# Start addresses of the token tiles inside SBUF: from a multiple of 128 bytes to 96 bytes past one

## The chip, the core and the metric

The kernel runs on one core of a Trainium2 chip. The time is the device time of one launch in microseconds (us), from all inputs in DRAM to the output in DRAM; three timed runs of the kernel before give 595.99 us (median; 595.70 to 596.36).

## What is computed

Sliding-window attention (window 64) over 2 x 8 heads of 576 tokens, then a dense mixture of four experts weighted by given probabilities, then a second mixture of eight experts of which each token uses one:

```python
attn = softmax(mask(q @ k.T / 8)) @ v                  # window of 64 tokens, head_dim 64
x = attn as (1152 tokens, 512)
for e in range(4):  out += p[:, e:e+1] * (relu(x @ w1[e]) @ w2[e])        # 512 -> 1024 -> 512
# second mixture: one expert of eight for each token
logits = out @ w_gate + modality_bias[modality_id]; e_idx = argmax(logits)
y[e_idx == e] = gate_w * (relu(out[e_idx == e] @ m2w1[e]) @ m2w2[e])
```

All inputs are float32.

## The kernel before

Every large product is done in three matmuls on values split in two float32r parts (a rounded high part and the rest): high by high, low by high, high by low. Such a product is called a triple here. The tokens lie transposed in two tiles, `xh` (high) and `xl` (low), each [128, 4, 1152]: four blocks of 128 features, 1152 tokens, 4608 bytes for one block's row in a partition. The weights of the expert in work lie in the tiles `wh0` to `wh7` and `wl0` to `wl7` (0 to 3: first layer, 4 to 7: second), 4096 bytes each in a partition; the rows of the first layer's output lie in `hh` and `hl`, [128, 8, 384].

The first layer (`mm1_part`, line 343) streams tokens through TensorE: the stationary operand is a 128-column piece of a weight tile, the moving operand is `xh` or `xl` at one feature block and 256, 352 or 384 tokens. One output block of 128 takes four triples, that is 12 matmuls, in one PSUM bank; ScalarE and VectorE then make `hh` and `hl` of it (lines 352 and 353). The second layer (`mm2_part`, line 368) has 128 (or 96) rows of `hh` or `hl` as the stationary operand and 512 columns of a second-layer weight tile as the moving operand; it doesn't touch `xh` or `xl`.

The program has these stages: attention for 18 blocks of 64 tokens in each sequence, into whose TensorE work the first tokens of expert 0 are mixed (0 to 155 us); the groups of 384 tokens of experts 1 to 3, first layer then second layer (155 to 452 us); the routed slots of 256 and 352 tokens (to the end), whose tokens are gathered, turned and written into `xh` and `xl` again (`turn`, lines 1030 to 1035). The attention writes `xh` and `xl` at lines 330 and 335. In one early piece (`g0_mm`, line 499, 24 matmuls) `xh` and `xl` are the stationary operand.

Tiles are placed one behind the other in each partition, in the order in which a pool first names them, rounded up to 32 bytes. `const` comes first and holds `ident`, `mk`, `prob` and `psumw`; `big` follows with `xh`, `xl`, `hh`, `hl`, `acc` and `ident4`; then `wp` with the weights. Where a tile begins is thus set by the sizes of those ahead of it; the odd widths of `psumw` (24 floats for 9) and `ident4` (56 for 32) are of that kind.

Of the kernel before, what the change touches and what calls it, by code (L numbers as in the profile page):

```python
# [5 lines left out]
F32 = mybir.dt.float32  # L6
# [9 lines left out]
def build(tc, q, k, v, probs, w1, w2, mid, wg, mbias, m2w1, m2w2, out):  # L16
# [4 lines left out]
    NTILE = NT // 128  # L21
# [7 lines left out]
    with ctx:  # L29
        const = ctx.enter_context(tc.tile_pool(name="const", bufs=1))  # L30
        big = ctx.enter_context(tc.tile_pool(name="big", bufs=1))
# [10 lines left out]
        ident = const.tile([128, 128], F32, name="ident")  # L42
        mk = const.tile([128, 3, 128], F32, name="mk")
        prob = const.tile([128, NTILE, E], F32, name="prob")
        psumw = const.tile([128, 24], F32, name="psumw")[:, 0:NTILE].rearrange("p (t o) -> p t o", o=1)
        xh = big.tile([128, HP, NT], F32R, name="xh")
        xl = big.tile([128, HP, NT], F32R, name="xl")
        hh = big.tile([128, KF, GT], F32R, name="hh")
        hl = big.tile([128, KF, GT], F32R, name="hl")
        acc = big.tile([128, NTILE, 520], F32, name="acc")  # L50

        ident4 = big.tile([128, 56], F32, name="ident4")[:, 0:32]

        with tc.manual_schedule():

# [7 lines left out]
            for i2, own in ((0, 0), (1, 1)):  # L63
                a = mk[64 * i2:64 * i2 + 64]
                o, p_ = a[:, :, 64 * own:64 * own + 64], a[:, :, 64 - 64 * own:128 - 64 * own]
# [131 lines left out]
            def unit_of(n):  # L197
                u, hp = divmod(n, HP)
                return units[u] + (u, hp)
# [403 lines left out]
            for n in range(NA):  # L603
                t, nb, u, hp = unit_of(n)
# [676 lines left out]
```

## Time and profile before

| | us |
|---|---|
| median of three runs | 595.99 |
| the profiled execution, its own time | 595.89 |
| its span, first to last instruction | 594.1 |
| TensorE busy in the span | 585.4 (99%) |
| VectorE, ScalarE, GpSimd busy | 248.6, 192.1, 83.4 |
| first-layer matmuls, line 343 | 1632 |
| second-layer matmuls, line 368 | 1104 |

TensorE is busy nearly the whole span. A matmul's busy time in the rows holds its latency too, and matmuls overlap, so the sum of their durations is far over the span; what one costs in a dense stretch is the distance from its start to the next one's start, called its pitch here. Rows of a timeline give starts to 0.01 us, so a pitch is read over several matmuls.

### The profile page before, as it was taken

The numbers are of one execution on the slowest core, as the hardware profiler recorded it, in microseconds if no ns is written. First come the engines' busy times: TensorE is split into PE (matmuls) and PEld (weight loads), VectorE is DVE, ScalarE is ACT, GpSimd is POOL, SyncE is SP. The second block draws the span as 40 slices with busy tenths as digits, with TensorE's granted clock in tenths as the row PEclk, the third lists the DMA queues.
The fourth block names the chain that finished last, engine by engine and source line by source line (L and its number), as shares of the span: only waits on it lengthen the run. The fifth ranks groups of instructions, "written<-read, shape, count | busy, mean of one in ns | idle before, by whom it ended". The sixth has DMA issues, their size and how long they took to land. (4 is left out here: it accounts for less than half of the span.)

```text
span 594.1 us, 9420 instructions
## 1 busy us (share of the span) xinstructions
PE 585.4 (99%) x3818; PEld 517.0 (87%) x3818; DVE 248.6 (42%) x534; ACT 192.1 (32%) x373; POOL 83.4 (14%) x129
## 2 busy tenths in 40 slices
PE   8999999999999999999999999999999999999996
PEld 7798797979898989899898989899898989897964
DVE  4954545363462212524121243335168597233410
ACT  5853434352340101313020222222043455233421
POOL 3851212022000000000000000000002105323221
PEclk9999999999999999999999999999999999999999
DMA  8996460000521000224000040002306277316530
GB/s 212 201 254 99 89 196 1 2 2 1 143 76 68 0 1 0 75 67 135 9 0 1 1 142 1 0 1 69 127 2 203 79 269 210 133 54 207 189 90 31
DMA packets 55919, 51.11 MB, mean 86 GB/s; under 512 B 41151, under 2 KB 41151, under 8 KB 55872
## 3 DMA queue, kind: packets, MB, share of 16 engines
q1 hardware_dynamic: 53664, 45.05, 27.7%
q0 software_dynamic: 1680, 5.29, 2.6%
q8 instruction: 31, 0.51, 0.4%
q10 hardware_dynamic: 528, 0.13, 0.1%
q14 instruction: 16, 0.13, 0.1%
HBM read 45.71 MB, written 4.95 MB: 85 GB/s over the span
## 5 line engine op out<-in xcount | busy, mean ns | idle before, releaser
L343 PE MATMUL ps<-xh,wh 128*128 128x384 f32 (+2 forms) x544 | 173.5, 319 | 0.0
L343 PE MATMUL ps<-xh,wl 128*128 128x384 f32 (+2 forms) x544 | 171.7, 316 | 0.0
L343 PE MATMUL ps<-xl,wh 128*128 128x384 f32 (+2 forms) x544 | 171.5, 315 | 0.0
L368 PE MATMUL ps<-wh,hh 128*128 128x512 f32 (+1 forms) x368 | 147.2, 400 | 0.3 <-DVE hl L353 0.3
L368 PE MATMUL ps<-wh,hl 128*128 128x512 f32 (+1 forms) x368 | 144.0, 391 | 0.0
L368 PE MATMUL ps<-wl,hh 128*128 128x512 f32 (+1 forms) x368 | 143.8, 391 | 0.0
L352 ACT ACTIVATE hh<-ps 128x384 fp32r<-128x384 f32 (+2 forms) x112 | 52.0, 464 | 260.4 <-PE ps L343 255.8
L353 DVE SCALAR_TENSOR_TENSOR hl<-ps,hh 128x384 fp32r<-128x384 f32 (+2 forms) x112 | 58.2, 522 | 118.6 <-ACT hh L352 118.6
L343 PEld LDWEIGHTS ps<-xh,wh 128*128 128x128 f32 x544 | 103.0, 189 | 0.9 <-issue 0.3
L343 PEld LDWEIGHTS ps<-xl,wh 128*128 128x128 f32 x544 | 103.0, 189 | 0.5
L343 PEld LDWEIGHTS ps<-xh,wl 128*128 128x128 f32 x544 | 102.9, 189 | 0.0
L368 PEld LDWEIGHTS ps<-wh,hh 128*128 128x128 f32 (+1 forms) x368 | 68.8, 187 | 16.7 <-issue 2.2
L368 PEld LDWEIGHTS ps<-wh,hl 128*128 128x128 f32 (+1 forms) x368 | 68.7, 187 | 15.3
L368 PEld LDWEIGHTS ps<-wl,hh 128*128 128x128 f32 (+1 forms) x368 | 68.8, 187 | 13.3
L379 DVE SCALAR_TENSOR_TENSOR acc<-ps,prob,acc 128x512 f32<-128x512 f32 x27 | 20.3, 750 | 94.9 <-PE ps L368 94.9
L1019 POOL DMA_INDIRECT xr<-x2d,idg x11 | 12.5, 1137 | 317.5 <-DVE ids L730 314.9
L171 DVE TENSOR_TENSOR wl<-raw,wh 128x1024 fp32r<-128x1024 f32 x42 | 52.0, 1253 | 8.8 <-ACT wh L167 8.8
L167 ACT ACTIVATE wh<-raw 128x1024 fp32r<-128x1024 f32 x48 | 49.1, 1052 | 0.0
L277 ACT ACTIVATE sm<-sm,st 128x128 f32<-128x128 f32 x72 | 23.2, 391 | 5.4 <-DVE st L266 5.4
L294 POOL TENSOR_TENSOR sm<-sm,rs 128x512 f32<-128x512 f32 (+1 forms) x20 | 19.5, 976 | 26.3 <-DVE rs L287 24.3
L257 DVE SCALAR_TENSOR_TENSOR sm<-psS,mk 128x256 f32<-128x256 f32 (+1 forms) x40 | 14.0, 391 | 19.0 <-PE psS L245 17.7
L1042 POOL DMA_INDIRECT out_dram<-y,ids x11 | 11.3, 1024 | 58.5 <-ACT y L1040 37.2
(189 smaller groups left out, 413.1 us busy)
## 6 DMA issues: line engine op xcount, KB each, us to landing
raw<-in_moe_w_dram SPq DMA_DIRECT2D x60, 512.0 KB, 4.0
x2d<-acc SPq DMA_DIRECT2D x3, 780.0 KB, 3.8
va<-in_v_dram SPq DMA_DIRECT2D x8, 256.0 KB, 5.1
vb<-in_v_dram SPq DMA_DIRECT2D x16, 128.0 KB, 4.5
acc<-in_moe_w_dram SPq DMA_DIRECT2D x4, 512.0 KB, 8.6
acc<-in_q_dram SPq DMA_DIRECT2D x6, 128.0 KB, 4.3
qu<-in_q_dram SPq DMA_DIRECT2D x3, 256.0 KB, 4.0
ku<-in_k_dram SPq DMA_DIRECT2D x3, 256.0 KB, 4.8
```

The source lines that it names most:

```text
L167: nc.scalar.activation(out=hi, in_=x, func=ACTF.Copy)
L171: eng.tensor_tensor(out=lo[:, o], in0=x[:, o], in1=hi[:, o].bitcast(F32), op=ALU.subtract)
L257: nc.vector.scalar_tensor_tensor(out=p[:, h], in0=ps[:, h, 0:128 * nj].rearrange("p (j c) -> p j c", j=nj), scalar=0.125, in1=m, op0=ALU.m ...
L277: nc.scalar.activation(out=p[:, h, j], in_=p[:, h, j], func=ACTF.Exp, bias=st[:, o:o + 1])
L294: nc.gpsimd.tensor_tensor(out=p, in0=p, in1=rs.rearrange("p (h j) o -> p h j o", h=2).to_broadcast([128, 2, nj, 128]), op=ALU.mult)
L343: nc.tensor.matmul(out=ps[:, 0:n], lhsT=a[kk][:, fs], rhs=b_[:, kk, gs], start=(kk == 0 and term == 0) if first is None else (first and te ...
L352: nc.scalar.activation(out=hi, in_=ps[:, 0:n], func=ACTF.Relu)
L353: nc.vector.scalar_tensor_tensor(out=lo, in0=ps[:, 0:n], scalar=0.0, in1=hi.bitcast(F32), op0=ALU.max, op1=ALU.subtract)
L368: nc.tensor.matmul(out=ps[0:m], lhsT=a[:, f, ts_], rhs=b_[c][:, o:o + 512], start=(f == 0 and i == 0), stop=(f == KF - 1 and i == 2))
L379: nc.vector.scalar_tensor_tensor(out=o, in0=ps, scalar=prob[:, t, e:e + 1], in1=o, op0=ALU.mult, op1=ALU.add)
L1019: nc.gpsimd.indirect_dma_start(out=x, out_offset=None, in_=x2d[0:last, :], in_offset=bass.IndirectOffsetOnAxis(ap=idg[i][:, a:a + 1], axis=0))
L1042: nc.gpsimd.indirect_dma_start(out=out, out_offset=bass.IndirectOffsetOnAxis(ap=ap, axis=0), in_=y[0:m], in_offset=None, bounds_check=NT - ...
```

## The change

No instruction is added, removed or moved: the lists of instructions of the two programs have the same operations, shapes, waits and order on every engine. Four lines change sizes of tiles, or the place of `ident4`, and with them the addresses. Byte offsets of the tiles in a partition, and what is left of them after the last multiple of 128:

| tile | before | rest | after | rest |
|---|---|---|---|---|
| xh | 18816 | 0 | 18912 | 96 |
| xl | 37248 | 0 | 37344 | 96 |
| hh | 55680 | 0 | 55936 | 0 |
| hl | 67968 | 0 | 68224 | 0 |
| acc | 80256 | 0 | 80512 | 0 |
| ident4 | 98976 | 32 | 55776 | 96 |
| wh0 (the other 15 follow, 4096 apart) | 99200 | 0 | 99328 | 0 |

All tiles behind the weights move on by 128 bytes, as they do. Inside `xh` and `xl` a feature block is 36 times 128 bytes and a group of tokens begins at a multiple of 128 tokens, so every first-layer matmul's moving operand begins at a multiple of 128 before, and 96 bytes past one after. Modulo 512 all of `xh`, `xl`, `hh`, `hl` and the weights begin at the same place (384) before; after, `xh` and `xl` begin at 480, `hh` and `hl` at 128, the weights at 0.

```diff
-        psumw = const.tile([128, 24], F32, name="psumw")[:, 0:NTILE].rearrange("p (t o) -> p t o", o=1)
+        psumw = const.tile([128, 48], F32, name="psumw")[:, 0:NTILE].rearrange("p (t o) -> p t o", o=1)
         xh = big.tile([128, HP, NT], F32R, name="xh")
         xl = big.tile([128, HP, NT], F32R, name="xl")
+
+        ident4 = big.tile([128, 40], F32, name="ident4")[:, 0:32]
         hh = big.tile([128, KF, GT], F32R, name="hh")
         hl = big.tile([128, KF, GT], F32R, name="hl")
-        acc = big.tile([128, NTILE, 520], F32, name="acc")
-
-        ident4 = big.tile([128, 56], F32, name="ident4")[:, 0:32]
+        acc = big.tile([128, NTILE * 520 + 24], F32, name="acc")[:, 0:NTILE * 520].rearrange("p (t d) -> p t d", d=520)
```

Tiles that already begin off a multiple of 128 in the kernel before are useful for reading the rows: token tile t of `acc` begins 32 t bytes past one (2080 bytes each), the gathered rows `xr` begin at 0, 32, 64 or 96 past one, `fewy` at 64 past one, the four feature blocks of `wgb` that line 767 streams at 0, 48, 96 and 16 past one.

## Rows read from the trace of the kernel before

**Rows 1.** The page: span, and busy time, share and instructions of each engine.

```profile
span 594.1 us, 9420 instructions
PE 585.4 (99%) x3818; PEld 517.0 (87%) x3818; DVE 248.6 (42%) x534; ACT 192.1 (32%) x373; POOL 83.4 (14%) x129
```

**Rows 2.** Waits of TensorE: who, for whom, us in total, times, longest.

```profile
PE psW L80 <- POOL ident L57: 1.4, 1, 1.4
PE psX L303 <- POOL sm L294: 0.6, 1, 0.6
PE psS L245 <- DVE sm L257: 0.5, 2, 0.3
PE ps L368 <- DVE hl L353: 0.3, 1, 0.3
```

**Rows 3.** Groups by shape, TensorE: operands, count, busy us, mean ns, idle before.

```profile
L368 PE MATMUL ps<-wh,hh 128*128 128x512 f32 x352 | 140.8, 400 | 0.3 <-DVE hl L353 0.3
L343 PE MATMUL ps<-xh,wh 128*128 128x384 f32 x288 | 97.5, 339 | 0.0
L343 PE MATMUL ps<-xh,wh 128*128 128x256 f32 x192 | 55.3, 288 | 0.0
L343 PE MATMUL ps<-xh,wh 128*128 128x352 f32 x64 | 20.8, 325 | 0.0
```

**Rows 4.** Windows, line 343: length, busy and count of PE and PEld, clock, DMA.

```profile
163.09:177.65 14.56, 14.56 (x85) 14.40 (x84) 1.00 0.29 76
```

**Rows 5.** Timeline of TensorE, 256 tokens then 352 tokens: start us, us, what.

```profile
38.76 0.28 PE L343 MATMUL ps<-xh,wl 128*128 128x256 f32 x1
...
41.64 0.28 PE L343 MATMUL ps<-xh,wl 128*128 128x256 f32 x1
...
517.54 0.32 PE L343 MATMUL ps<-xh,wh 128*128 128x352 f32 x1
...
521.41 0.32 PE L343 MATMUL ps<-xh,wh 128*128 128x352 f32 x1
...
529.57 0.32 PE L343 MATMUL ps<-xh,wh 128*128 128x352 f32 x1
...
531.49 0.39 PE L368 MATMUL ps<-wh,hh 128*128 128x512 f32 x1
```

**Rows 6.** Timeline of TensorE in a second layer, 512 columns.

```profile
385.82 0.39 PE L368 MATMUL ps<-wh,hl 128*128 128x512 f32 x1
...
387.18 0.39 PE L368 MATMUL ps<-wh,hl 128*128 128x512 f32 x1
```

**Rows 7.** Single lines: engine, operation, count, duration ns min/median/max, first and last start.

```profile
L1136 PE MATMUL psF<-acc,xg x16: 592/593/617, 564.8 to 566.2; 128*32 128x512 f32 x16
L1164 PE MATMUL psF<-fewy,ident x2: 592/604/617, 577.7 to 578.1; 128*32 128x512 f32 x2
L767 PE MATMUL psGL<-wgb,xg x108: 172/173/188, 399.4 to 474.5; 128*128 128x24 bf16 x108
L751 PE MATMUL psGT<-ident,acc x36: 270/273/308, 394.3 to 469.8; 128*128 128x128 f32 x36
```

**Rows 8.** Single lines: loads of stationary operands, VectorE on `acc`, writes of token tiles.

```profile
L751 PEld LDWEIGHTS psGT<-ident,acc x36: 138/140/143, 394.1 to 469.7; 128*128 128x128 f32 x36
L1030 PEld LDWEIGHTS psT<-ident,xr x40: 138/139/144, 460.1 to 539.0; 128*128 128x128 f32 x40
L379 DVE SCALAR_TENSOR_TENSOR acc<-ps,prob,acc x27: 745/751/752, 183.3 to 467.7; 128x512 f32<-128x512 f32 x27
L343 PEld LDWEIGHTS ps<-xh,wh x544: 186/188/203, 35.9 to 564.1; 128*128 128x128 f32 x182
L335 DVE TENSOR_TENSOR xl<-psO,xh x20: 259/424/425, 17.0 to 139.0; 128x256 fp32r<-128x256 f32 x16, 128x128 fp32r<-128x128 f32 x4
L1034 ACT ACTIVATE xh<-psT x10: 591/598/600, 461.0 to 539.4; 128x512 fp32r<-128x512 f32 x10
```

**Rows 9.** Timeline of TensorE: a first-layer matmul, then transposes of `acc`, tiles 0 and 3.

```profile
394.10 0.34 PE L343 MATMUL ps<-xh,wl 128*128 128x384 f32 x1
394.28 0.60 PE L751 MATMUL psGT<-ident,acc 128*128 128x128 f32 x4
...
429.86 0.34 PE L343 MATMUL ps<-xh,wl 128*128 128x384 f32 x1
430.03 0.60 PE L751 MATMUL psGT<-ident,acc 128*128 128x128 f32 x4
```

## The prediction

> **What bounds the kernel now.** I read the page first: TensorE is busy 585.4 of 594.1 us, VectorE 248.6, ScalarE 192.1 [rows 1]. Then the waits of TensorE: four pairs, 2.8 us in all, and none of them a first-layer matmul [rows 2]. So the end follows TensorE's own pace, and a nanosecond on a matmul is a nanosecond on the time. The groups by shape name the two big users, line 368 with 512 columns and line 343 with 384, 256 and 352 [rows 3]; their mean durations (400, 339, 288 and 325 ns) contain latency that the next matmul covers, so I take pitches instead. For 384 tokens, 84 matmuls fill 14.56 us: 173.3 ns, at a granted clock of 1.00, the 2.4 GHz level [rows 4]. For 256 tokens, 24 matmuls stand between the first two rows of [rows 5]: 2.88 us / 24 = 120.0 ns. For 512 columns, 6 matmuls in 1.36 us: 226.7 ns [rows 6]. At 2.4 GHz the columns alone are 160.0, 106.7 and 213.3 ns. What is left is the same each time, **13.3 ns**, whatever the width and whichever layer: it is a cost per matmul, not per column, and equals 32 columns, or 128 bytes of a float32r row. For 352 tokens (columns alone 146.7 ns) there are two paces: 24 matmuls in 3.87 us, 161.3 ns, and later, in the same slot and on the same addresses, 12 in 1.92 us, 160.0 ns, again 13.3 over the columns [rows 5].
>
> **The change, part by part.** *Instructions*: none is added, removed or moved, no queue is passed, no wait is new. What changes is where operands start: the moving operand of all 1632 first-layer matmuls (544 triples), the outputs of the instructions that write `xh` and `xl`, and the stationary operand of 24 early matmuls. `hh`, `hl`, `acc`, the weights and everything behind stay on the same rest modulo 128.
>
> *Writes into the token tiles.* 30 on ScalarE and 30 on VectorE over the whole program (20 at lines 330 and 335 each, 10 at lines 1034 and 1035 each) [rows 8]. The nearest row is line 379: its 27 instructions read and write `acc` tiles that begin 0, 32, 64 and 96 past a multiple of 128, and all of them take 745 to 752 ns [rows 8]. At most 7 ns each, so 60 x 7 ns = 0.4 us if all of it were on the path; most of it lies beside TensorE. I take 0. The bound below is -0.4 us by the same row.
>
> *Stationary operands.* 36 loads from `acc` tiles at four rests take 138 to 143 ns, 40 loads from gathered rows at four rests 138 to 144 ns [rows 8]. So 24 x 6 ns = 0.1 us at most, hidden beside the matmul before. I take 0.
>
> *The moving operand*, the term that decides. No row shows a float32r stream that begins off a multiple of 128, so I bound it. From near: line 1164 streams 512 float32 columns from `fewy`, 64 past a multiple, and takes 592 and 617 ns; line 1136 streams 512 from `acc`, on a multiple, and takes 592 to 617 ns [rows 7]: equal at both ends, difference 0. Line 767 streams from four starts, 0, 16, 48 and 96 past a multiple, and its 108 matmuls have one median, 173 ns [rows 7]; these are only 24 bf16 columns, so that row is weak. The first row is stronger, but a plain float32 stream takes two passes and so may have slack that a float32r stream at one column a cycle lacks. From far: the 13.3 ns is the only fixed cost that rows show. It could double (one more piece of 32 columns: +13.3 ns) or fall to what the transposes show. Four of them, 128 columns in two passes (106.7 ns), fill 0.60 us [rows 9], of which the last one takes 0.27 [rows 7]: 0.33 us for three steps, a pitch of 110 ns, 3.3 ns over the columns. That would be -10.0 ns. So the term lies between 1632 x -10.0 ns = **-16.3 us** and 1632 x +13.3 ns = **+21.8 us**. I take **0**, by line 1164, the only row with a long stream off the multiple.
>
> *Relative place of moving and stationary operand.* All large tiles begin at the same place modulo 512 before; afterwards a first-layer stream begins 480 past its weights. One row has that very distance: the matmul at 429.86 streams `xh` while `acc` tile 3 is loaded for the transposes, 480 apart modulo 512, and the next start is 0.17 us later; at 394.10, before `acc` tile 0 with the same start modulo 512, it is 0.18 us [rows 9]. No difference beyond the rows' 0.01 us. I take 0 here too. For the second layer (1104 matmuls) the distance changes by 128 and the rest modulo 128 does not; I take 0.
>
> *Sum*: 595.89 us for the profiled execution (594.1 of span and 1.8 around it) + 0 + 0 + 0 = 595.9, against a median of 595.99 in the timed runs. I predict 596.0.
>
> **Rivals.** *One more piece (slower).* The constant equals 128 bytes for four widths, all of them multiples of 32 columns. If a stream is fetched in pieces of a fixed grid, and the constant is the piece that must be there ahead, a stream that begins 96 past a grid line touches one piece more. With 128-byte pieces that is 13.3 ns on each of 1632 matmuls, +21.8 us, 617.7; with 64-byte pieces half, +10.9 us, 606.8. For it: the exactness of the constant. Against it: line 1164 at 64 past shows nothing [rows 7]. It decides as soon as the 384 pitch exceeds 173.3 by 0.75 ns, since 1632 x 0.75 ns is 1.2 us. By the Trainium skill (SBUF — State Buffer, Specifications (TRN2)) the lines are of 16 bytes, and 96 bytes are six whole ones, so this rival would be worth nothing; no row here shows the size of a line.
>
> *The pace slips (slower, small).* At 352 tokens the stream can stay at 161.3 ns instead of 160.0 [rows 5]. So the 13.3 is a state into which the stream of loads and the stream of columns fall, and not always. If an odd start keeps the other widths out of it in the same way, 1440 matmuls x 1.3 ns = 1.9 us: 597.9. For it: those two paces. Against it: the 256 and 384 streams hold theirs, and 352 found it too after a break.
>
> *The constant shrinks (faster).* If the 13.3 ns comes from loads and streams that begin on the same place modulo 512 and get in each other's way, then moving the tokens apart frees part of it: down to the transposes' 3.3 ns it is -16.3 us, 579.6; half of it, 587.7. For it: a load of 188 ns runs beside every first-layer matmul, one of 140 beside a transpose [rows 8], and the transpose has the smaller rest. Against it: the distance of 480 in [rows 9], which didn't help. The Trainium skill (TensorE: Matmul & The Clock Gate, Back-to-back issue gap) states N/2.4 + 2.5 ns for a matmul alone, which is an estimate of 10.8 ns less than the rows have, and by it the gain could be 17.6 us and the time 578.3; but the same page (Step-by-step: what each phase is for) gives loads a read port of their own, by which they take nothing from the stream.
>
> **How the numbers follow.** No effect: 0.48, 595.5 to 596.5. The pace slips: 0.12, near 597.9. One more piece: 0.19, of which 0.10 for the half (606.8) and 0.09 for the whole (617.7). The constant shrinks: 0.21, of which 0.11 for half (587.7) and 0.10 for the whole (579.6). The range leaves out both whole cases, 0.19, and takes in the half ones with the 0.4 us of the writes and the spread of the runs: 587 to 609. The likeliest case alone would be 595.5 to 596.5. Less than 0.2%, 1.2 us, is about what a measurement of this kernel can't tell from no change: so faster 0.21, same 0.48, slower 0.12 + 0.19 = 0.31.
>
> **What would show it.** In the trace after, the pitch of first-layer matmuls decides: 173.3 ns at 384 tokens and 120.0 at 256 if I am right, 180 to 187 and 127 to 133 for one more piece, 163 to 168 and 110 to 115 if the constant shrinks, and about 174.6 and 121.3 where the pace slips. The second layer is the control, 226.7 ns: if it moves, it is not the start of the tokens that matters but the distance of the tiles. TensorE's waits should stay near 2.8 us; if they grow, the writes into the token tiles got slower, which I hold for the least likely of all. I am wrong if a pitch moves although line 1164 didn't feel its start, which would mean that a one-pass stream has no slack for it.

## The result: 0.6% slower, by the second layer

The changed kernel takes 599.61 us (median of four runs, 598.88 to 600.12) against 595.88 for the kernel before: a ratio of 1.006, 95% interval 1.0043 to 1.0078. That is slower by 3.7 us, on a forecast of no effect (596.0) with a range of 587 to 609.

The page after, the lines that answer to [rows 1], and then TensorE's waits (who, for whom, us in total, times, longest), which answer to [rows 2]:

```profile
span 598.3 us, 9420 instructions
PE 589.6 (99%) x3818; PEld 517.2 (86%) x3818; DVE 248.6 (42%) x534; ACT 192.2 (32%) x373; POOL 83.4 (14%) x129
```

```profile
PE psW L80 <- POOL ident L57: 1.4, 1, 1.4
PE psX L303 <- POOL sm L294: 0.6, 1, 0.6
PE psS L245 <- DVE sm L257: 0.5, 2, 0.3
PE ps L368 <- DVE hl L353: 0.4, 1, 0.4
```

The instructions are the same, and the busy time of VectorE, ScalarE and GpSimd and the waits are the same to 0.1 us. Only TensorE is busy 4.2 us longer, the whole of the span's growth. The groups of TensorE after (line, operands, count, then busy us and mean ns), and behind them two groups of the page before, say which matmuls:

```profile
L343 PE MATMUL ps<-xh,wh 128*128 128x384 f32 (+2 forms) x544 | 173.6, 319 | 0.0
L343 PE MATMUL ps<-xl,wh 128*128 128x384 f32 (+2 forms) x544 | 171.5, 315 | 0.0
L343 PE MATMUL ps<-xh,wl 128*128 128x384 f32 (+2 forms) x544 | 171.2, 315 | 0.0
L368 PE MATMUL ps<-wh,hh 128*128 128x512 f32 (+1 forms) x368 | 148.6, 404 | 0.4 <-DVE hl L353 0.4
L368 PE MATMUL ps<-wh,hl 128*128 128x512 f32 (+1 forms) x368 | 145.3, 395 | 0.0
L368 PE MATMUL ps<-wl,hh 128*128 128x512 f32 (+1 forms) x368 | 145.1, 394 | 0.0
```

```profile
L368 PE MATMUL ps<-wh,hh 128*128 128x512 f32 (+1 forms) x368 | 147.2, 400 | 0.3 <-DVE hl L353 0.3
L368 PE MATMUL ps<-wh,hl 128*128 128x512 f32 (+1 forms) x368 | 144.0, 391 | 0.0
```

The first layer, whose tokens were moved by 96 bytes, is where it was to 0.5 us in these rows. The second layer, which touches neither token tile, is slower in all three terms: its mean is 394 to 404 ns for 391 to 400 before. In dense stretches (runs of matmuls with nothing else between them) the pitch shows it plainly. The windows of the kernel after (length, then busy time and count of TensorE and of its loads; first a second layer of 60 matmuls, then first layers of 84 with 384 tokens and 84 with 256; TensorE's count holds a neighbour or two that overlap the edge):

```profile
214.48:228.43 13.95, 13.95 (x61) 11.12 (x59) 1.00 0.01 1
197.14:211.70 14.56, 14.56 (x85) 14.40 (x84) 1.00 0.00 0
140.50:150.44 9.94, 9.94 (x86) 9.90 (x84) 1.00 0.01 2
```

The same second layer and the same first layer of 256 tokens in the kernel before:

```profile
213.44:227.04 13.60, 13.60 (x61) 11.08 (x59) 1.00 0.00 1
140.00:150.07 10.07, 10.07 (x86) 10.03 (x84) 1.00 0.01 2
```

13.95 us / 60 = **232.5 ns**, against 13.60 / 60 = 226.7 before, as in [rows 6]; 14.56 / 84 = 173.3 ns, the same as [rows 4]; 9.94 / 84 = 118.3 ns, against 120.0 in [rows 5]. Summed from start to start over all rows of the two traces, line 368 grew by 4.6 us (4.1 ns on each of 1104 matmuls; the pitch in stretches that are cut by other matmuls grew less), line 343 shrank by 1.0 us (256 tokens -0.8, 352 -0.2, 384 -0.05), and the first layer began 0.6 us later, a delay that arose in the first 15 us, while the inputs come in. 4.6 - 1.0 + 0.6 = 4.2 us, the growth of the span. The last part may be of that one execution alone: the medians differ by 3.7 us, and in the traces of the other kernels the first layer begins anywhere from 35.3 to 36.6 us.

So the start of the tokens did not cost anything where it was looked for, and something that the change moved on the way did: `hh` and `hl` by 256 bytes, the weights by 128. Both stay on multiples of 128, but modulo 256 the second layer's moving operand (a weight tile) now begins 128 past its stationary one (`hh` or `hl`), where before the two began on the same place.

### The profile page after: what moved, and what is told of

Its sections match the earlier page's. It is cut to its first block, busy times and chain, and to the rows that moved or that the text cites. A ratio compares the mean times of both kernels' runs of the same rounds, so it can differ in the third digit from the quotient of the medians.

```text
span 598.3 us, 9420 instructions
## 1 busy us (share of the span) xinstructions
PE 589.6 (99%) x3818; PEld 517.2 (86%) x3818; DVE 248.6 (42%) x534; ACT 192.2 (32%) x373; POOL 83.4 (14%) x129
## 5 line engine op out<-in xcount | busy, mean ns | idle before, releaser
L171 POOL TENSOR_TENSOR wl<-raw,wh 128x1024 fp32r<-128x1024 f32 x6 | 14.4, 2408 | 34.7 <-ACT wh L167 34.7
```

The source lines that it names most:

```text
L171: eng.tensor_tensor(out=lo[:, o], in0=x[:, o], in1=hi[:, o].bitcast(F32), op=ALU.subtract)
```

## Experiments: distance or start?

Two theories. **A**: the pace goes by the distance between the starts of a matmul's moving and stationary operand, modulo some power of two up to 512. **B**: it goes by where a tile itself begins. All kernels below compute the same with the same instructions; they differ from the kernel before in padding alone, and each diff shows only the lines that change. A distance is the start of the moving operand less that of the stationary one: tokens less weights in the first layer, weights less `hh` in the second.

**Tokens alone.** `xh` and `xl` at 96 past a multiple of 128, everything else as before modulo 512.

```diff
-        psumw = const.tile([128, 24], F32, name="psumw")[:, 0:NTILE].rearrange("p (t o) -> p t o", o=1)
+        psumw = const.tile([128, 48], F32, name="psumw")[:, 0:NTILE].rearrange("p (t o) -> p t o", o=1)
-        xl = big.tile([128, HP, NT], F32R, name="xl")
+        xl = big.tile([128, 4608 + 104], F32R, name="xl")[:, 0:4608].rearrange("p (a b) -> p a b", b=1152)
```

> xh and xl begin 96 past a multiple of 128 as in the changed kernel, and hh, hl and all weights begin at the same place modulo 512 as in the kernel before (384). Theory A (the pace of a matmul depends on the distance, modulo 512 or less, between the start of its moving and of its stationary operand; the changed kernel lost because its hh and its weights ended 128 bytes apart): second-layer pitch back at 226.7 ns, first layer as in the changed kernel or near it (256 tokens about 118, 384 about 173.5), time 594.3 to 595.5, a little under before. Theory B (the start of the token tiles itself slows the program, through whatever it shares with the second layer): second-layer pitch 232 as in the changed kernel, 599 to 600.

Measured: 597.99 us, ratio 1.0035 (1.0021 to 1.0048). Windows, a second layer of 60 matmuls, then a first layer of 84 with 384 tokens:

```profile
214.28:227.88 13.60, 13.60 (x61) 11.07 (x59) 1.00 0.01 1
196.69:211.53 14.84, 14.84 (x85) 14.67 (x84) 1.00 0.00 0
```

The second layer is back at 226.7 ns, as A said and B denied. But the first layer at 384 tokens runs at 14.84 / 84 = 176.7 ns, which neither foresaw: I had taken its distance for that of the changed kernel. It isn't: 480 - 384 = 96 here, 480 - 0 = 480 there. That the same tokens at the same place run at 173.3 in one kernel and 176.7 in the other is a point for A, if a weak one: further down one kernel shows both paces at one distance. The time missed the 594.3 to 595.5 that A was to give, by this first layer.

**Rows and weights apart, tokens at home.**

```diff
-        xl = big.tile([128, HP, NT], F32R, name="xl")
+        xl = big.tile([128, 4608 + 64], F32R, name="xl")[:, 0:4608].rearrange("p (a b) -> p a b", b=1152)
-        ident4 = big.tile([128, 56], F32, name="ident4")[:, 0:32]
+        ident4 = big.tile([128, 152], F32, name="ident4")[:, 0:32]
```

> xh and xl begin where they did before; hh and hl begin at 128 modulo 512 and the weights at 0, as in the changed kernel. Theory A: second layer 231 to 233 ns, +4 to +5 us; the first layer now has its tokens 384 past its weights modulo 512, that is 128 apart, and if 128 apart is what costs there too, its pitches also rise by about 4 ns x 1632 = +6.5 us: 600 to 607. Theory B: as before, 595.9.

Measured: 601.30 us, ratio 1.0092 (1.0077 to 1.0108). The second layer of 60, and the first of 84 with 384 tokens:

```profile
214.20:228.20 14.00, 14.00 (x61) 11.08 (x59) 1.00 0.00 1
196.62:211.40 14.78, 14.78 (x85) 14.61 (x84) 1.00 0.00 0
```

233.3 ns in the second layer, as A expected, and 176.0 in the first, 2.7 ns more where about 4 were thought possible; the tokens hadn't moved modulo 512. Without the tokens' shift the loss is there all the same.

**Everything 96 past.** One number moves all large tiles by 96 bytes.

```diff
-        psumw = const.tile([128, 24], F32, name="psumw")[:, 0:NTILE].rearrange("p (t o) -> p t o", o=1)
+        psumw = const.tile([128, 48], F32, name="psumw")[:, 0:NTILE].rearrange("p (t o) -> p t o", o=1)
```

> Every large tile (xh, xl, hh, hl, acc, all weights, the raw buffers) begins 96 past a multiple of 128, at 480 modulo 512; all distances are 0 as in the kernel before. Theory A: the same as before, 595.5 to 596.4, pitches 120.0, 173.3 and 226.7. Theory B, or any rule by which a start off a multiple of 128 costs something by itself: slower by 4 us or more.

Measured: 596.08 us, ratio 1.0001 (0.9992 to 1.0010). Second layer, first layer of 384 and of 256 tokens:

```profile
213.99:227.59 13.60, 13.60 (x61) 11.07 (x59) 1.00 0.00 1
196.67:211.23 14.56, 14.56 (x85) 14.40 (x84) 1.00 0.00 0
140.55:150.63 10.08, 10.08 (x86) 10.03 (x84) 1.00 0.01 2
```

226.7, 173.3 and 120.0 ns, those of before. No large tile begins on a multiple of 128 any more, and nothing is lost. Theory B falls: the weights begin at 480 modulo 512 here, and at the same 480 in the kernel with 448 and 96 below, whose rows begin at 384 and whose second layer runs at 233.2 ns.

**Only `hh` and `hl` moved, by 128.**

```diff
-        xl = big.tile([128, HP, NT], F32R, name="xl")
+        xl = big.tile([128, 4608 + 32], F32R, name="xl")[:, 0:4608].rearrange("p (a b) -> p a b", b=1152)
-        ident4 = big.tile([128, 56], F32, name="ident4")[:, 0:32]
+        ident4 = big.tile([128, 152], F32, name="ident4")[:, 0:32]
```

> Only hh and hl (and acc behind them) move by 128 modulo 512, to 0; tokens and weights stay at 384, so the second layer's moving operand begins 384 past its stationary one as in the changed kernel, with every start on a multiple of 128, and the first layer keeps distance 0. Theory A: second layer 231 to 233 ns, first layer 120.0 and 173.3, time 595.9 + 1104 x 4.2 ns = 600.5 (599.5 to 601.5). If it is the place of the weights (0 modulo 512 in the changed kernel) that costs and not the distance: as before, 595.9.

Measured: 600.24 us, ratio 1.0072 (1.0058 to 1.0086).

```profile
213.94:227.89 13.95, 13.95 (x61) 11.12 (x59) 1.00 0.01 1
196.60:211.16 14.56, 14.56 (x85) 14.40 (x84) 1.00 0.00 0
```

232.5 ns in the second layer, the same as in the changed kernel, and the first layer untouched at 173.3. Modulo 512 the moving operands stand where they stood; of the two layers' operands the second layer's stationary one alone was moved, from one multiple of 128 to the next. (`acc`, which lies behind it, went along; but in the kernel with 32 and 480 below the weights alone move, and the second layer loses as much.) This is the loss of the changed kernel, reproduced by itself.

## Experiments: which distances

**256 and 256.** The weights alone move, by 256 bytes.

```diff
-        ident4 = big.tile([128, 56], F32, name="ident4")[:, 0:32]
+        ident4 = big.tile([128, 120], F32, name="ident4")[:, 0:32]
```

> Weights 256 past the rows hh, hl and the tokens modulo 512: both layers at distance 256 (moving start less stationary start). If the distance counts modulo 256 or less: as at distance 0, pitches 120.0, 173.3, 226.7 and 595.9. If it counts modulo 512: other pitches in both layers, by the spread seen so far (-3 to +5 ns) between 593 and 602.

Measured: 595.68 us, ratio 0.9999 (0.9989 to 1.0009). Second layer of 60, first layer of 84 with 256 tokens: 226.7 and 120.1 ns. A distance of 256 is as good as one of 0, so the distances are given modulo 256 from here on where they are compared; no other pair that differs by 256 was tried by itself.

```profile
213.08:226.68 13.60, 13.60 (x61) 11.07 (x59) 1.00 0.01 1
139.63:149.72 10.09, 10.09 (x86) 10.04 (x84) 1.00 0.01 2
```

The kernels that follow vary the same paddings; the pair of numbers ahead of each is the distance in the first and in the second layer.

**64 and 64**.

```diff
-        psumw = const.tile([128, 24], F32, name="psumw")[:, 0:NTILE].rearrange("p (t o) -> p t o", o=1)
+        psumw = const.tile([128, 56], F32, name="psumw")[:, 0:NTILE].rearrange("p (t o) -> p t o", o=1)
-        xl = big.tile([128, HP, NT], F32R, name="xl")
+        xl = big.tile([128, 4608 + 96], F32R, name="xl")[:, 0:4608].rearrange("p (a b) -> p a b", b=1152)
-        ident4 = big.tile([128, 56], F32, name="ident4")[:, 0:32]
+        ident4 = big.tile([128, 72], F32, name="ident4")[:, 0:32]
```

> Both layers at distance 64. Seen so far: first layer at 384 tokens 173.3 (distance 0), 173.7 (480), 176.7 (96), 175.9 (384); second layer 226.7 (0) and 232 (384). If any distance off 0 costs: first layer near 175, second layer 229 to 233, 599 to 602. If the collision is of two streams on one place at one time, a distance of half a 128-byte piece could also take away part of the 13.3 ns: pitches under 173.3 and 226.7, under 595.

Measured: 597.70 us, ratio 1.0031 (1.0018 to 1.0043). The second layer runs at 14.00 / 60 = 233.3 ns in the long groups, but 39 matmuls of its first group take 8.93 us, 229.0 ns, and in the routed slots it comes near that again: at this distance it too has two paces. 256 tokens: 117.7 ns. The three windows in the order of this paragraph:

```profile
212.63:226.63 14.00, 14.00 (x61) 11.15 (x59) 1.00 0.00 1
150.83:159.76 8.93, 8.93 (x40) 7.14 (x38) 1.00 0.60 183
138.88:148.77 9.89, 9.89 (x86) 9.85 (x84) 1.00 0.01 2
```

**32 and 480**.

```diff
-        ident4 = big.tile([128, 56], F32, name="ident4")[:, 0:32]
+        ident4 = big.tile([128, 48], F32, name="ident4")[:, 0:32]
```

> First layer at distance 32, second layer at 480 (the tokens' distance in the changed kernel). If the two layers follow one rule, the second layer at 480 should show what the first did there: nearly nothing (226 to 228). First layer at 32: unknown, 172 to 177 at 384 tokens. 594 to 599.

Measured: 598.73 us, ratio 1.0050 (1.0033 to 1.0066). The second layer at 480 runs at 14.00 / 60 = 233.3 ns, where the first layer in the changed kernel hardly moved: the two layers, which differ in width too, don't share one table of good and bad distances, and this expectation was wrong.

```profile
213.06:227.06 14.00, 14.00 (x61) 11.08 (x59) 1.00 0.00 1
```

**448 and 96**.

```diff
-        psumw = const.tile([128, 24], F32, name="psumw")[:, 0:NTILE].rearrange("p (t o) -> p t o", o=1)
+        psumw = const.tile([128, 32], F32, name="psumw")[:, 0:NTILE].rearrange("p (t o) -> p t o", o=1)
-        xl = big.tile([128, HP, NT], F32R, name="xl")
+        xl = big.tile([128, 4608 + 120], F32R, name="xl")[:, 0:4608].rearrange("p (a b) -> p a b", b=1152)
-        ident4 = big.tile([128, 56], F32, name="ident4")[:, 0:32]
+        ident4 = big.tile([128, 80], F32, name="ident4")[:, 0:32]
```

> First layer at distance 448, second layer at 96. If the two layers follow one rule, the second layer at 96 costs about 3 ns as the first did there (230, +3.3 us). First layer at 448: unknown, 172 to 177 at 384 tokens. 597 to 602.

Measured: 598.55 us, ratio 1.0040 (1.0026 to 1.0054). The second layer runs at 233.2 ns, where 230 was expected; the first layer at 256 tokens at 9.53 / 84 = **113.4 ns**, 6.6 under the kernel before: a distance can give as well as take.

```profile
139.59:149.12 9.53, 9.53 (x86) 9.49 (x84) 1.00 0.01 2
```

**192 and 0**, the version that should beat both (192 is 448 modulo 256).

```diff
-        psumw = const.tile([128, 24], F32, name="psumw")[:, 0:NTILE].rearrange("p (t o) -> p t o", o=1)
+        psumw = const.tile([128, 72], F32, name="psumw")[:, 0:NTILE].rearrange("p (t o) -> p t o", o=1)
-        xl = big.tile([128, HP, NT], F32R, name="xl")
+        xl = big.tile([128, 4608 + 80], F32R, name="xl")[:, 0:4608].rearrange("p (a b) -> p a b", b=1152)
```

> First layer at distance 192 (modulo 256 the same as 448, where 256-token matmuls ran at 114), second layer at 0. If the period is 256 and the two layers are independent: 256 tokens 7.7 ns over the columns in place of 13.2, 576 x 5.5 ns = 3.2 us less, 352 tokens 0.8 x 192 = 0.2 us less, 384 tokens and second layer as before: 592.5 (592.0 to 593.3), faster than both kernels by more than the noise. If it was something else than the distance that made 448 fast: 595.9.

Measured: 595.37 us, ratio 0.9989 (0.9980 to 0.9998). Faster than the changed kernel by far and than the kernel before by 0.6 us, hardly more than the noise, and not the 3.4 us of the expectation. Windows: a first layer of 84 with 384 tokens, then 48 matmuls of 256 tokens in one place and 48 in another of the same kernel:

```profile
193.97:208.81 14.84, 14.84 (x85) 14.68 (x84) 1.00 0.00 0
109.27:114.71 5.44, 5.44 (x51) 5.44 (x49) 1.00 0.00 0
141.87:147.53 5.66, 5.66 (x51) 5.66 (x49) 1.00 0.01 3
```

At 256 tokens it came (113.3 ns, and 117.9 in the other place; -2.5 us summed over the trace). At 384 it went again: 176.7 ns in every unbroken group, +2.1 us, although 448 modulo 256 had shown 173.3 there. So the distance isn't the whole: one distance can have several paces.

**192 and 192**.

```diff
-        psumw = const.tile([128, 24], F32, name="psumw")[:, 0:NTILE].rearrange("p (t o) -> p t o", o=1)
+        psumw = const.tile([128, 120], F32, name="psumw")[:, 0:NTILE].rearrange("p (t o) -> p t o", o=1)
-        xl = big.tile([128, HP, NT], F32R, name="xl")
+        xl = big.tile([128, 4608 + 32], F32R, name="xl")[:, 0:4608].rearrange("p (a b) -> p a b", b=1152)
-        ident4 = big.tile([128, 56], F32, name="ident4")[:, 0:32]
+        ident4 = big.tile([128, 104], F32, name="ident4")[:, 0:32]
```

> First layer at 192 again, second layer at 192, not seen yet. First layer as in the kernel with 192 and 0 (7.7 over the columns for 256 tokens). Second layer 231 to 233 if every distance off 0 costs: 592.5 + 4.5 to 5.5 = 597 to 598; under 226.7 if a distance helps the second layer as it helps the first.

Measured: 598.34 us, ratio 1.0044 (1.0028 to 1.0059). First layer of 84 with 384 tokens, second layer of 60:

```profile
195.44:210.00 14.56, 14.56 (x85) 14.40 (x84) 1.00 0.00 0
212.79:226.79 14.00, 14.00 (x61) 11.09 (x59) 1.00 0.01 1
```

The same first-layer distance as in the kernel with 192 and 0, and 173.3 ns in place of 176.7. What differs, beside the absolute places, is the pace of the second layer that runs between two first layers.

**160 and 32**.

```diff
-        psumw = const.tile([128, 24], F32, name="psumw")[:, 0:NTILE].rearrange("p (t o) -> p t o", o=1)
+        psumw = const.tile([128, 72], F32, name="psumw")[:, 0:NTILE].rearrange("p (t o) -> p t o", o=1)
-        xl = big.tile([128, HP, NT], F32R, name="xl")
+        xl = big.tile([128, 4608 + 80], F32R, name="xl")[:, 0:4608].rearrange("p (a b) -> p a b", b=1152)
-        ident4 = big.tile([128, 56], F32, name="ident4")[:, 0:32]
+        ident4 = big.tile([128, 64], F32, name="ident4")[:, 0:32]
```

> First layer at 160, second layer at 32, both not seen yet. By the neighbours 128 and 192 the first layer should be at 8 to 12 ns over the columns for 256 tokens and 13.7 to 16 for 384; the second layer, if every distance off 0 costs it 4 to 5 ns, at 231 to 233: 597 to 600. If the second layer has a good distance as the first has, under 226.7.

Measured: 600.22 us, ratio 1.0065 (1.0050 to 1.0080); second layer 233.2. Two groups of 384 tokens in this one kernel, 48 matmuls each, the first group and the second:

```profile
169.88:178.36 8.48, 8.48 (x49) 8.48 (x49) 1.00 0.39 124
203.49:211.81 8.32, 8.32 (x50) 8.32 (x49) 1.00 0.00 0
```

176.7 ns, then 173.3 in this and all later unbroken groups: same tiles, same addresses modulo 256, same instructions. The first window also has transfers beside it (a DMA share of 0.39 against 0.00), but those alone don't set the pace: 24 matmuls of the fourth group run beside a share of 0.41 and take 4.16 / 24 = 173.3 ns, and the kernel with 192 and 0 ran at 176.7 beside a share of 0.00. Nor does the pace of the second layer ahead: the 48 matmuls ahead of the first group and the 72 ahead of the second take 11.20 and 16.80 us, 233.3 ns each. These three windows:

```profile
267.91:272.07 4.16, 4.16 (x25) 4.16 (x25) 1.00 0.41 122
150.38:161.58 11.20, 11.20 (x48) 8.81 (x48) 1.00 0.52 152
178.54:195.34 16.80, 16.80 (x72) 13.31 (x72) 1.00 0.17 58
```

So a pace, once taken, is held through a group, and what a stream takes depends on something at its entry that these runs don't name.

**64 and 160**.

```diff
-        psumw = const.tile([128, 24], F32, name="psumw")[:, 0:NTILE].rearrange("p (t o) -> p t o", o=1)
+        psumw = const.tile([128, 80], F32, name="psumw")[:, 0:NTILE].rearrange("p (t o) -> p t o", o=1)
-        xl = big.tile([128, HP, NT], F32R, name="xl")
+        xl = big.tile([128, 4608 + 72], F32R, name="xl")[:, 0:4608].rearrange("p (a b) -> p a b", b=1152)
-        ident4 = big.tile([128, 56], F32, name="ident4")[:, 0:32]
+        ident4 = big.tile([128, 96], F32, name="ident4")[:, 0:32]
```

> First layer at 64, as before in another kernel: 256 tokens 10.7 over the columns again, 384 tokens 13.3, whatever the second layer's distance. Second layer at 160, not seen yet: 231 to 233 if every distance off 0 costs. 597 to 599.

Measured: 600.28 us, ratio 1.0074 (1.0058 to 1.0089). Second layer 14.05 / 60 = 234.2, the slowest seen; 256 tokens at 113.4 in one place, where the other kernel with 64 had 117.7; the expectation had 117.4 whatever the second layer does.

```profile
213.41:227.46 14.05, 14.05 (x61) 11.11 (x59) 1.00 0.01 1
139.69:149.22 9.53, 9.53 (x86) 9.49 (x84) 1.00 0.01 2
```

The paces together, in ns, from the dense stretches; where kernels or groups differ, the paces seen stand side by side:

| distance modulo 256 | second layer, 512 | first layer, 384 | first layer, 256 |
|---|---|---|---|
| 0 | 226.7 | 173.3 | 120.0 |
| 32 | 233.2 | 173.3 | 116.7, 117.8 |
| 64 | 229.0, 233.3 | 173.3 | 113.4, 117.8 |
| 96 | 233.2 | 176.7 | 120.0 |
| 128 | 232.5, 233.3 | 175.5, 176.0 | 118.8 |
| 160 | 234.2 | 173.3, 176.7 | 117.3, 118.7 |
| 192 | 233.3 | 173.3, 176.7 | 113.4, 117.8 |
| 224 | 233.3 | 173.3 | 118.3 |

## Why the prediction was right in its range and wrong in its middle

The measured 599.61 us lies in the range of 587 to 609, but that is luck: the range reached up there for a first layer with half a piece more, at 606.8, and the time came from a second layer that the sum had at 0. The sign to look for was well chosen: it made the second layer the control and said that, if it moved, the distance of the tiles mattered and not the start of the tokens.

*What bounds the kernel*: right. TensorE's waits stayed at 2.9 us, and a few nanoseconds on a matmul came out as microseconds on the time.

*Writes, stationary starts of the 24 early matmuls*: right, 0 within what can be read; VectorE and ScalarE are busy for the same time, and the kernel with every tile 96 past a multiple runs at 596.08. The 24 early matmuls, whose distance changed from 0 to 32 modulo 256, took the same 6.35 us before as after, to 0.02 us.

*The start of the moving operand, taken as 0*: right as a statement on starts, and now shown for float32r streams that begin 96 past, by the kernel with everything at 96. Line 1164 [rows 7] spoke of starts alone, and there it held. The rival of one more piece is dead: it would have given 606.8 or 617.7 there.

*Relative place of moving and stationary operand*: **this is the step that failed**, in its last sentence, "the distance changes by 128 and the rest modulo 128 does not; I take 0". The second layer grew by 4.6 us; moving `hh` and `hl` by 128 alone makes the kernel 4.3 us slower (600.24 against 595.98) with the same 232.5 ns. No dense float32r stream in the trace of before had another distance than 0, so that trace couldn't show this, and the term should have been bounded by the rows with two paces and not taken at 0; even that bound, 1104 x 1.3 ns = 1.4 us, would have been a third of what came. The row that I leaned on for the first layer [rows 9] was no evidence, and I misread it: `acc` tile 3 begins at 480 modulo 512 and the stream beside it at 384, so their distance is 384 - 480, that is 416, and not the changed kernel's 480. It is also a single matmul, where a pace is a matter of many in a row: the 24 early matmuls, in short runs between others, show nothing of their new distance.

*The pace slips*: this rival had a part of what happened, a pace that is left for a slower one, with the wrong stream, the wrong trigger (an odd start) and under a quarter of the size. The two paces at 352 tokens were the one sign in the trace of before that the 13.3 ns over the columns is a state and not a constant. I priced a slip at 1.3 ns, from that row, and gave it to the first layer; it came in the second, 5.8 ns in dense stretches. That 597.9 is the rival nearest to the measured time is chance.

*The constant shrinks*: at 256 tokens it does, from 13.3 to 11.7 ns in the changed kernel and to 6.7 at the best distance. At 384 and 512 no distance brought it under 13.3. The Trainium skill gives loads a read port of their own, by which they take nothing from the stream (TensorE: Matmul & The Clock Gate, Step-by-step: what each phase is for). That doesn't settle the time here: moving only the stationary operand by 128 bytes changed the stream's pitch from 226.7 to 232.5 ns. The N/2.4 + 2.5 ns that the Trainium skill states for a matmul alone (TensorE: Matmul & The Clock Gate, Back-to-back issue gap) isn't reached by any dense float32r stream of these runs; the least is 6.7 ns over the columns.

What stays open: by what the place of the stationary operand acts on the pace of the stream, and what picks the pace on entry. It is shown that the second layer's pace hangs on the distance of its two operands and not on where either begins, and that groups alike in addresses can hold two paces. That reads collide is one reading of it, which no run here tests. What lets the first layer enter at 173.3 with 192 and 192, and not with 192 and 0, wasn't tried by itself; a slower second layer ahead is not enough, since with 160 and 32 the group behind one of 233.3 ns ran at 176.7.

## What to carry over

In a kernel that TensorE bounds, padding a tile moves all tiles behind it, and with them the distance modulo 256 bytes between the moving and the stationary operand of every matmul; look at all pairs, not at the tile that was moved. Start from operands on one place modulo 256, which in dense stretches was the best for 512 columns and no worse than any for 384, and test another distance on the chip, matmul shape by matmul shape, reading pitches from start to start, since durations and waits barely show it. Whether a start is a multiple of 128 was of no account by itself: 596.08 us with every large tile 96 past one, 595.98 before.

## What the runs showed of the hardware that was not expected

Dense float32r streams settle into few paces. The commonest are 113.3, 116.7 and 120.0 ns for 256 columns, 173.3 and 176.7 for 384, 226.7 and 233.3 for 512. Over the columns at 2.4 GHz these are 16, 24 and 32, 32 and 40, 32 and 48 columns: multiples of 8 columns, or 32 bytes, each time. There are others between them (117.8, 118.3, 176.0, 229.0, 232.5). A pace is a mean: at 232.5 in the changed kernel the single steps go from 228 to 241 ns in a pattern that repeats. And one kernel, on one set of addresses modulo 256, can hold two of them in different places, 176.7 and 173.3 ns in two groups of the same instructions, and neither the transfers beside them nor the pace of the second layer ahead is enough to tell the two apart.
